# The last blocks of a two-layer token kernel in 512 columns, its phase-A buffers moved to the far end of SBUF, and its short tail loads issued by GpSimd

## The chip, the core and the metric

One core of a Trainium2 chip runs the kernel. The metric is the device time of one execution in microseconds (us). Engines: PE is TensorE (matmuls; PEld is its weight load), DVE is VectorE, ACT is ScalarE, POOL is GpSimd, SP is SyncE, which here only issues DMAs.

## What is computed

```python
def _attn_ref(q, k, v, omega):          # q, k, v: (4, 8, 576, 64); omega: (128, 64)
    scale = 1.0 / np.sqrt(np.sqrt(D))
    def phi(x):
        proj = np.einsum('bhsd,md->bhsm', x, omega)
        h = proj - np.sum(x * x, axis=-1, keepdims=True) / 2.0
        h = h - np.max(h, axis=-1, keepdims=True)
        return np.exp(h) / np.sqrt(m)
    q_p, k_p = (phi(q * scale), phi(k * scale))
    kv = np.einsum('bhsm,bhsd->bhmd', k_p, v)
    z = np.sum(k_p, axis=2)
    num = np.einsum('bhsm,bhmd->bhsd', q_p, kv)
    den = np.einsum('bhsm,bhm->bhs', q_p, z)[..., None] + 1e-06
    return num / den
# x: the attention output as 2304 tokens x 512
x = (x @ w_a) * (x @ w_b) @ w_out       # 512 -> 1536 -> 512   (phase A)
h = np.maximum(x @ w_in, 0.0)
out = h * h @ w_out2                    # 512 -> 2048 -> 512   (phase B)
```

Weights arrive as 64-bit floats; the kernel splits each into a high and a low fp32r part on ACT and DVE, does the same with the activations, and takes three products (high-high, high-low, low-high) for each matmul.

## The kernel before

**Attention.** Per batch of 576 tokens and pair of heads, 512 tokens are taken as four chunks of 128 (`Side`, `k_steps`, `q_steps`), and the last 64, the tail, of four heads at a time apart (`kt_steps`, `qt_steps`; tiles `kt`, `qt`, `VT`). `tail_load` and `kt_steps` issue four DMAs of 32 KB for each tail tile of a batch: twelve such sets, 48 DMAs, all on SP's queue. `kt_steps` runs ahead of the two `k_steps` of its group; `kv_tail` is added to each. The lanes of attention are cut into steps and woven (`merge`, `chain`, `SIDES`) into phase A's units, and a scheduler then orders each engine's instructions by their place in the program.

**Phase A** (`a_units`) works on nine blocks of N = 256 tokens. A unit (block, f), with f one of FA = 12 slices of 128 of the 1536 features, has 12 matmuls into one half of a PSUM bank for `w_a` (three terms times KC = 4 slices of 512), 12 into the other half for `w_b`, the product on ACT and DVE (`a_s`, `gs`: lines 599 to 602), and, LAG = 2 units later, 12 matmuls of `w_out` into the two `y` banks (`outs`, line 562). `PASSES` lists the order: blocks 0 to 2 by halves of f, blocks 3 to 6 whole, and the last two blocks, 7 and 8, by halves again, so that half of the first-layer weights is done with, and their slots can take second-layer weights, before phase A ends. A half pass parks its sum in DRAM (`y_d`) and the next reads it back (`prefetch`, `y_p`).

**Second-layer weights** (`get_w2`) are 32 tiles: each a 512 KB load (`raw`, two buffers), five DVE and three ACT instructions (`split`), into a slot. 20 of them are made during the last four passes, 12 in phase B's first two passes.

**Phase B** (`b_units`) takes the same nine blocks of 256. For each of FB = 16 slices f: 12 matmuls `ph` of 256 columns (line 673), relu, square and split on ACT and DVE (lines 680 to 683), and, LAGB = 2 slices later, per 128 tokens three matmuls `o` whose moving operand is the 512 columns of `wo2` (line 661), six for a block. So `ph`, `ab` and `y` stream 256 columns, and `o` streams 512. The last rows are copied out on ACT (`o_s`) and stored.

## Time and profile before

| | |
|---|---|
| median of 3 executions | 1091.64 us (1089.7 to 1091.91) |
| the profiled execution | 1089.11 us, span from first to last instruction 1087.3 us |
| mean granted TensorE clock | 0.997 |
| PE busy | 1056.3 us, 7705 matmuls |
| DVE, ACT busy | 575.8 us, 514.0 us |
| 40 slices, busy tenths, PE | 5998999999999999999999999999999999999998 |
| the same, DVE | 4888887666655433454467877623333323333322 |
| matmuls `ab`, `ph`, `o`, `y` | 2592, 1728, 864, 1296 |

Each digit is the busy share of a fortieth of the span in tenths. Busy spans of PE overlap since matmuls are pipelined, so a full digit doesn't mean that PE is at its fastest: what one matmul costs in a stream is the distance from one start to the next.

### The profile page before, as it was taken

The page shows a single profiled execution, that of the slowest core. Times are in us where ns is not written, and L with a number is a line of the kernel's source. Part 1 is how long each engine was busy: PE and PEld are TensorE (multiplying, and loading weights), DVE is VectorE, ACT ScalarE, POOL GpSimd, SP SyncE. Part 2 cuts the span into 40 slices and gives each one's busy share as a digit, 9 for nine tenths or more (in the row PEclk, how much of TensorE's full clock was granted, in tenths as well). Part 3 has the DMA queues.
Part 4 walks back from the last instruction along what each step waited for, and adds up shares of the span by engine and source line. Part 5 has one row for each costly group of instructions (what it writes and reads, how often), then busy time and mean ns, then how long its engine had stood idle before and what let it go on. Part 6 is the DMA issues. An engine that isn't in the chain of part 4 may idle for free.

```text
span 1087.3 us, 19942 instructions
## 1 busy us (share of the span) xinstructions
PE 1056.3 (97%) x7705; PEld 991.1 (91%) x7705; DVE 575.8 (53%) x1700; ACT 514.0 (47%) x1321; POOL 0.7 (0%) x6
## 2 busy tenths in 40 slices
PE   5998999999999999999999999999999999999998
PEld 3797989999999999999999998999999999999997
DVE  4888887666655433454467877623333323333322
ACT  4887767654465533433346654523332323323232
POOL 0000000000000000000000000000000000000000
...
GB/s 138 195 200 175 236 255 186 237 201 88 156 132 95 97 135 112 127 98 113 121 136 266 276 285 258 78 1 40 39 28 12 40 1 39 20 2 20 1 20 20
DMA packets 109630, 127.19 MB, mean 117 GB/s; under 512 B 62176, under 2 KB 82656, under 8 KB 109536
## 3 DMA queue, kind: packets, MB, share of 16 engines
...
q8 instruction: 61, 1.00, 0.4%
...
## 4 chain that ended last, share of the span: by engine, by line
PE 88%; DMA 3%; DVE 3%; ACT 3%; issue 1%; SPq 1%; ACTq 0%
PE ab L548 25%; PE ph L673 19%; PE o L661 18%; PE y L562 12%; PE ps_p L289 3%; PE ps_p L222 3%; PE ps_kv L356 2%; PE ps_n L413 2%; PE ps_qt L405 2%; DMA raw<-in_moe_w_out_dram 2%; PE ps_t L267 1%; DVE u L138 1%; PE ps_x L423 1%; ACT a L124 1%; DVE p L129 1%
## 5 line engine op out<-in xcount | busy, mean ns | idle before, releaser
L548 PE MATMUL ab<-x,w 128*128 128x256 f32 x2592 | 368.4, 289 | 1.3 <-ACT x L485 1.3
L548 PEld LDWEIGHTS ab<-x,w 128*128 128x128 f32 x2592 | 332.3, 192 | 2.9 <-ACT x L485 1.5
L673 PEld LDWEIGHTS ph<-yx,w 128*128 128x128 f32 x1728 | 223.8, 192 | 10.0
L673 PE MATMUL ph<-yx,w 128*128 128x256 f32 x1728 | 226.8, 283 | 0.0
L661 PE MATMUL o<-w,ss 128*128 128x512 f32 x864 | 219.0, 393 | 0.0
L562 PE MATMUL y<-gs,wo 128*128 128x256 f32 x1296 | 187.9, 290 | 2.8 <-ACT gs L601 2.2
L661 PEld LDWEIGHTS o<-w,ss 128*128 128x128 f32 x864 | 154.5, 189 | 26.5
L562 PEld LDWEIGHTS y<-gs,wo 128*128 128x128 f32 x1296 | 167.5, 192 | 4.2 <-ACT gs L601 2.6
L681 DVE TENSOR_TENSOR r<-r 128x256 f32<-128x256 f32 x144 | 61.3, 426 | 199.1 <-ACT r L680 196.7
L680 ACT ACTIVATE r<-ph 128x256 f32<-128x256 f32 x144 | 55.5, 385 | 186.5 <-PE ph L673 186.5
L683 DVE TENSOR_TENSOR ss<-r,ss 128x256 fp32r<-128x256 f32 x144 | 61.4, 426 | 63.2 <-PE o L661 48.8
L682 ACT CAST ss<-r 128x256 fp32r<-128x256 f32 x144 | 58.7, 408 | 65.4 <-DVE r L681 65.4
L599 ACT ACTIVATE a_s<-ab 128x256 f32<-128x256 f32 x108 | 41.4, 383 | 90.4 <-PE ab L548 90.2
L600 DVE TENSOR_TENSOR a_s<-ab,a_s 128x256 f32<-128x256 f32 x108 | 45.4, 420 | 45.8 <-ACT a_s L599 45.1
L124 ACT ACTIVATE a<-raw 128x512 f32<-128x512 f32 x68 | 46.4, 683 | 30.9 <-DMA raw<-in_moe_w_in_dram 9.9
L601 ACT CAST gs<-a_s 128x256 fp32r<-128x256 f32 x108 | 44.0, 408 | 28.8 <-DVE a_s L600 28.1
L296 DVE CUSTOM_DVE_ANT_0 c<-ps_p,c 128x128 f32<-128x128 f32 x160 | 39.7, 287 | 28.2 <-ACT c L294 27.8
L602 DVE TENSOR_TENSOR gs<-a_s,gs 128x256 fp32r<-128x256 f32 x108 | 45.5, 421 | 11.9 <-ACT gs L601 10.3
L138 DVE SCALAR_TENSOR_TENSOR u<-raw,u 128x512 uint32<-128x512 uint32 x68 | 46.6, 686 | 0.8 <-ACT u L134 0.3
L129 DVE SCALAR_TENSOR_TENSOR p<-a,p 128x512 int32<-128x512 int32 x68 | 46.7, 686 | 0.6
L134 ACT ACTIVATE u<-raw 128x512 int32<-128x512 uint16 x68 | 46.1, 678 | 0.0
L294 ACT COPY c<-ps_p 128x256 f32<-128x256 f32 x80 | 28.7, 372 | 35.1 <-PE ps_p L289 34.1
...
## 6 DMA issues: line engine op xcount, KB each, us to landing
...
y_d<-y_s SPq DMA_DIRECT2D x18, 256.0 KB, 4.5
yraw<-y_d SPq DMA_DIRECT2D x18, 256.0 KB, 2.9
```

Of the source, the lines that this page charges most:

```text
L124: nc.scalar.activation(out=a, in_=f32(up), func=ACTF.Copy, scale=WORD_SCALE)
L129: nc.vector.scalar_tensor_tensor(out=i32(p), in0=i32(a), scalar=-0x80000000, in1=i32(p), op0=ALU.bitwise_and, op1=ALU.bitwise_or,)
L134: nc.scalar.activation(out=i32(u), in_=raw.bitcast(U16)[:, :, 1], func=ACTF.Copy, scale=2.0 ** 7,)
L138: nc.vector.scalar_tensor_tensor(out=u.bitcast(U32), in0=up.bitcast(U32), scalar=23, in1=u.bitcast(U32), op0=ALU.logical_shift_left, op1=A ...
L548: nc.tensor.matmul(ps, lhsT=wv[:, s_, kc, :], rhs=x[:, kc, m_, :], start=(kc == 0 and (s_, m_) == TERMS[0]), stop=(kc == KC - 1 and (s_, m ...
L562: nc.tensor.matmul(y[c // 2][:, c % 2, :], lhsT=wo[pi, f][:, s_, c * 128:(c + 1) * 128], rhs=g[:, m_, :],  start=(f == f0 and c % 2 == 0 a ...
L661: nc.tensor.matmul(op[t], lhsT=s_t[f][:, s_, t * 128:(t + 1) * 128], rhs=wo2[f][:, m_, :], start=(f == 0 and (s_, m_) == TERMS[0]), stop=( ...
L673: nc.tensor.matmul(ps, lhsT=wv[:, s_, kc, :], rhs=y[:, kc, m_, :], start=(kc == 0 and (s_, m_) == TERMS[0]), stop=(kc == KC - 1 and (s_, m ...
L680: nc.scalar.activation(out=r, in_=ps, func=ACTF.Relu, scale=1.0 / W_SCALE)
L681: nc.vector.tensor_tensor(out=r, in0=r, in1=r, op=ALU.mult)
L682: nc.scalar.copy(out=s_t[f][:, 0, :], in_=r)
L683: nc.vector.tensor_tensor(out=s_t[f][:, 1, :], in0=r, in1=f32(s_t[f][:, 0, :]), op=ALU.subtract)
```

## The change

**Two blocks at once.** The last entry of `PASSES` is now one pass over blocks 7 and 8 together with all twelve f. Its matmuls stream 512 columns (`x_all[:, x0:x0 + 2]`); `w_a`, `w_b` and each of the four `y` parts have a PSUM bank of their own (banks 4 to 7 and 0 to 3), and `outs` follows one unit behind instead of two. The half passes of these blocks, with their parked sums, are gone. Phase B takes the blocks as `BB`: four of 512 columns and one of 256, `outs` one slice behind.

**Places.** `xpool`, `wop` and `gpool` lie at the right end of SBUF and close when phase A ends; `x_all` is one tile with three places instead of three buffers. `w2l`, `wide` and `yl` take the left end that attention leaves; `w2r` and `yr` take the right end after phase A. 27 of the 32 second-layer weights (`get_w2`) are made during the wide pass, most of them in first-layer slots as each f is done with, and five in phase B's first block.

**Tails.** The 48 tail DMAs are issued by GpSimd. `k_lane` runs `kt_steps` merged with the first `k_steps` of its group; the tail's product is added after that one, so ACT copies twice 130 columns where it copied 260 once.

```diff
+    pa = ExitStack()
+    xpool = pa.enter_context(tc.tile_pool(name="xpool", bufs=1, side="right"))
+    wop = pa.enter_context(tc.tile_pool(name="wop", bufs=3, side="right"))
+    gpool = pa.enter_context(tc.tile_pool(name="gpool", bufs=3, side="right"))
...
+    y_d = [
+        dram.tile([128, KC, min(2, NBLK - i) * N], F32, name=f"y_d{i // 2}")
+        for i in range(0, NBLK, 2)
+    ]
...
+    x_all = xpool.tile([128, 3, KC, 2, N], F32R, name="x_all")
 
     def x_tile(i):
-        if i not in xs:
-            xs[i] = xpool.tile([128, KC, 2, N], F32R, tag="x", name=f"x{i}")
-        return xs[i]
+        return x_all[:, i % 3]
...
-                    nc.sync.dma_start(
+                    nc.gpsimd.dma_start(
                         out=t[64 * e:64 * e + ST, g],
                         in_=src[b, h0:h0 + 2, SM:S, :].rearrange("h t d -> t h d"),
                     )
...
         st = tail_turn("k", b, g)
         yield
+        yield
         kp = ap1.tile([128, 2, M], F32, tag="kpt", name="kpt")
         phi_wide(st, kp)
         yield
+
+        while (b, g) not in kv_raw:
+            yield
         ps = at_bank([128, 2, 2, D + 1], "ps_kt")
         for h in range(2):
             nc.tensor.matmul(
                 ps[:, h].rearrange("p e d -> p (e d)"), lhsT=kp[:, h, :],
                 rhs=VT[:, g, h].rearrange("p e d -> p (e d)"), start=True, stop=True,
             )
-        t = ap2.tile([128, 2, 2, D + 1], F32, tag="kvt", name="kvt", bufs=1)
+        t = ap2.tile([128, 2, D + 1], F32, tag="kvt", name="kvt", bufs=1)
         kv_tail[b, g] = t
-        nc.scalar.copy(out=t, in_=ps)
-        kv_raw[b, g] = ap2.tile([128, 2, 2, D + 1], F32, tag="kvr", name="kvr", bufs=NP)
+        kv = kv_raw[b, g][:, :, 0, :]
+        nc.scalar.copy(out=t, in_=ps[:, :, 1, :])
+        nc.vector.tensor_tensor(out=kv, in0=ps[:, :, 0, :], in1=kv, op=ALU.add)
         yield
...
+        if e == 0:
+            kv_raw[b, g] = ap2.tile([128, 2, 2, D + 1], F32, tag="kvr", name="kvr", bufs=NP)
+            nc.scalar.copy(out=kv_raw[b, g][:, :, 0, :], in_=ps)
+        else:
+            nc.vector.tensor_tensor(
+                out=kv_raw[b, g][:, :, 1, :], in0=ps, in1=kv_tail[b, g], op=ALU.add
+            )
...
-            for x in ([(kt_steps(b, p // 2), 4)] if p % 2 == 0 else []) + [(k_steps(b, p), 7)]
+            for x in [merge((k_steps(b, p), 7), *([(kt_steps(b, p // 2), 7)] if p % 2 == 0 else []))]
...
-    PASSES += [(i, FH, FA) for i in (NBLK - 2, NBLK - 1)]
+    PASSES = [((i,), 0, FH) for i in range(3)] + [((i,), FH, FA) for i in range(3)]
+    PASSES += [((i,), 0, FA) for i in range(3, NBLK - 2)]
+    PASSES += [((NBLK - 2, NBLK - 1), 0, FA)]
     wa, wb, wo = {}, {}, {}
     LAG = 2
+    wide_pool = []
...
+            if wide:
+                for c in range(KC):
+                    t = ypool.tile([128, 2, N], F32, tag="ys", name="y_s")
+                    nc.scalar.mul(out=t, in_=yp[pi][c], mul=1.0 / W_SCALE ** 2)
+                    for x, i in enumerate(bl):
+                        nc.sync.dma_start(out=y_cols(i)[:, c, :], in_=t[:, x, :])
+                return
...
+            bl = PASSES[pi][0]
+            wide = len(bl) == 2
+            if wide:
+                x0 = bl[0] % 3
+                x = x_all[:, x0:x0 + 2]
+                aps, bps = (bank(4 + (2 * f + z) % 4, [128, 2, N], "abw") for z in range(2))
+                gp, w_ = wide_pool[0], 2 * N
+            else:
+                x = x_tile(bl[0])
+                ab = bank(2 + n % (2 if pi <= AT_END else 6), [128, 2, N], "ab")
+                aps, bps = ab[:, 0, :], ab[:, 1, :]
+                gp, w_ = gpool, N
+            proj(aps, wa[f], x)
             yield pi, f, "a"
-            proj(ab[:, 1, :], wb[f], x)
-            a_s = gpool.tile([128, N], F32, tag="t", name="a_s")
-            g = gpool.tile([128, 2, N], F32R, tag="gs", name="gs", bufs=3)
+            proj(bps, wb[f], x)
...
+            pending.append((pi, f))
+            while len(pending) > (1 if wide else LAG):
+                outs(*pending.pop(0))
             yield pi, f, "o"
-        for n in range(len(todo) - LAG, len(todo)):
-            outs(*todo[n])
+        for x in pending:
+            outs(*x)
...
+    BB = [(i * N, min(2, NBLK - i) * N) for i in range(0, NBLK, 2)]
+    ys = {}
+
+    def y_load(i, pool):
+        w_ = BB[i][1]
+        t = pool.tile([128, KC, 2, w_], F32R, tag="yx", name=f"yx{i}")
+        ys[i] = t
+        for c in range(KC):
+            r = ypool.tile([128, w_], F32, tag="ys", name="yraw")
+            nc.sync.dma_start(out=r, in_=y_d[i][:, c, :])
+            nc.scalar.copy(out=t[:, c, 0, :], in_=r)
...
+            for t in range(w_ // 128):
+                if f == 0:
+                    op[t] = bank(t, [128, DM], f"o{t}")
...
+        gp = wide_pool[0]
+        for f in range(FB):
+            ps = bank(4 + f % 4, [128, w_], "ph")
+            wv = wi2[f].rearrange("p a (k f) -> p a k f", k=KC)
+            for kc in range(KC):
...
+            r = gp.tile([128, w_], F32, tag="t", name="r")
+            s_t[f] = gp.tile([128, 2, w_], F32R, tag="gs", name="ss")
...
+            if f:
+                outs(f - 1)
             yield f
...
+        outs(FB - 1)
...
+    W2_L, W2_R = 3, 2 * (FB - FA) - 3
+    w2 = {"n": 0}
...
-        x, f = w2_list.pop(0)
-        po = (w2[0], "w2") if f < FB - FA else (wpool, "w")
+        w2["n"] += 1
+        x, f = w2_list[n]
+        if n < W2_L:
+            po = (w2["l"], "w2")
+        elif n < W2_L + 2 * FA:
+            po = (wpool, "w")
...
+            w2["l"] = ctx.enter_context(tc.tile_pool(name="w2l", bufs=W2_L))
+            wide_pool.append(ctx.enter_context(tc.tile_pool(name="wide", bufs=2)))
+            w2["yl"] = ctx.enter_context(tc.tile_pool(name="yl", bufs=1))
...
+            if w2["n"] < W2_L + 2 * f + (2 if kind != "a" else 0):
+                get_w2()
+            if f == 4 and kind == "o":
+                y_load(0, w2["yl"])
         u += 1
         while done < min(n_side, u * n_side / (n_units * FR.get(pi, 1.0))):
...
+        for f in b_units(i):
+            get_w2()
+            if f == (4 if i == 0 else FB - 6) and i + 1 < len(BB):
+                y_load(i + 1, w2["yl" if i % 2 else "yr"])
 
 
 # ---- launch: one core; inputs and outputs as the reference has them ----
```

What the scheduler makes of it, at three places. First SP's queue at the start of the program: `om` is omega, `kt` and `VT` are tails, `kn` and `V` the 512 tokens of a pair of heads, `raw` a weight. Before:

```order
L175 DMA om<-in_omega_dram 128x64
L176 DMA om<-in_omega_dram 128x64
L203 DMA kt<-in_k_dram 64x2x64 x4
L317 DMA VT<-in_v_dram 64x2x64 [waits DVE_49]
L317 DMA VT<-in_v_dram 64x2x64
L317 DMA VT<-in_v_dram 64x2x64 [waits DMAHW0_49]
L317 DMA VT<-in_v_dram 64x2x64 [waits DMAHW1_49]
L103 DMA raw<-in_moe_w_a_dram 128x4x256 [waits DMAHW2_49]
L247 DMA kn<-in_k_dram 128x8x64 [waits DMAHW3_49]
L342 DMA V<-in_v_dram 128x8x64 [waits DMAHW4_49]
```

Now:

```order
L179 DMA om<-in_omega_dram 128x64
L180 DMA om<-in_omega_dram 128x64
L251 DMA kn<-in_k_dram 128x8x64
L351 DMA V<-in_v_dram 128x8x64 [waits DVE_49]
L107 DMA raw<-in_moe_w_a_dram 128x4x256
L107 DMA raw<-in_moe_w_b_dram 128x4x256
L254 DMA qn<-in_q_dram 128x2x64 x2
```

The eight tail loads ahead of `raw` and `kn` have left SP's queue, and `kn` and `V` stand ahead of the first weights.

Second ACT's first instructions, where `OMS`, `OMZ` and `OM` are copies of the transposed omega, which every feature projection needs, and `S` and `T` are copies of transposed tokens and tails. Before:

```order
L187 ACT_TABLE_LOAD
L187 ACTIVATE OMS<-ps_om 128x128 [waits PE_49]
L190 ACTIVATE OMZ<-ps_om 64x128 [waits DVE_49]
L190 ACTIVATE OMZ<-ps_om 64x128
L191 CAST OM<-OMS 128x128 [waits Activation_49]
L215 COPY T<-ps_tt 128x128 [waits PE_49]
L124 ACTIVATE a<-raw 128x512 [waits DMAHW2_49]
L134 ACTIVATE u<-raw 128x512
L273 COPY S<-ps_t_176 128x512 [waits PE_49]
```

Now:

```order
L128 ACT_TABLE_LOAD
L128 ACTIVATE a<-raw 128x512 [waits DMAHW4_49]
L191 ACTIVATE OMS<-ps_om 128x128 [waits PE_49]
L194 ACTIVATE OMZ<-ps_om 64x128 [waits DVE_49]
L194 ACTIVATE OMZ<-ps_om 64x128
L195 CAST OM<-OMS 128x128 [waits Activation_49]
L138 ACTIVATE u<-raw 128x512
L277 COPY S<-ps_t_156 128x512 [waits PE_49]
L137 CAST w<-p 128x512 [waits DVE_49]
L219 COPY T<-ps_tt 128x128 [waits PE_49]
```

The scaling of the first weight, which waits for a DMA, now stands ahead of the copies of omega, and `S` ahead of `T`.

Third ACT's queue from phase A into phase B: `gs` and `ss` are the high parts that `y` and `o` of PE wait for, `y_s` copies a finished sum out of PSUM, `r` is the relu of `ph`. Before:

```order
L601 CAST gs<-a_s 128x256 [waits DVE_49]
L133 CAST w<-p 128x512 [waits DVE_49]
L124 ACTIVATE a<-raw 128x512 [waits DMAHW6_49]
L134 ACTIVATE u<-raw 128x512
L680 ACTIVATE r<-ph 128x256 [waits PE_49,Activation_49]
L124 ACTIVATE a<-raw 128x512 [waits DMAHW7_49,DVE_49]
L134 ACTIVATE u<-raw 128x512
L682 CAST ss<-r 128x256 [waits DVE_49]
```

Now:

```order
L597 ACTIVATE y_s<-y_8021 128x512 [waits PE_49]
L128 ACTIVATE a<-raw 128x512 [waits DMAHW1_49,DVE_49]
L597 ACTIVATE y_s<-y_8022 128x512 [waits PE_49]
L137 CAST w2r<-p 128x512 [waits DVE_49]
L138 ACTIVATE u<-raw 128x512
L137 CAST w2r<-p 128x512 [waits DVE_49]
L597 ACTIVATE y_s<-y_8023 128x512 [waits DMAHW2_49,DMAHW3_49,PE_49,Activation_49]
L723 ACTIVATE r<-ph 128x512 [waits PE_49]
L128 ACTIVATE a<-raw 128x512 [waits DMAHW4_49,DVE_49]
L138 ACTIVATE u<-raw 128x512
L597 ACTIVATE y_s<-y_8024 128x512 [waits DMAHW6_49,DMAHW5_49,Activation_49]
L725 CAST ss<-r 128x512 [waits DVE_49]
```

Four copies of sums, two of which wait for DMAs as well, now stand among the weight splits ahead of the first `ss`.

## Rows read from the trace of the kernel before

**Rows 1.** Engines by stage: stretch, length, busy us (instructions) of each, clock, DMA share.
```profile
0.00:12.24 12.24, 0.89 (x2) 0.36 (x3) 2.52 (x7) 3.74 (x8) 0.70 (x6) 1.00 0.49 110
12.24:190.00 177.76, 166.09 (x1193) 151.15 (x1194) 148.11 (x437) 135.12 (x368) 0.00 (x0) 0.99 0.72 204
...
561.00:676.85 115.85, 113.07 (x926) 112.06 (x925) 91.54 (x190) 70.47 (x142) 0.00 (x0) 0.99 0.81 265
676.85:1083.00 406.15, 406.15 (x2594) 369.54 (x2593) 140.93 (x323) 135.76 (x329) 0.00 (x0) 1.00 0.08 25
```

**Rows 2.** Timeline of PE in phase B: start, us from first start to last end.
```profile
898.71 4.27 PE L661 MATMUL o<-w,ss 128*128 128x512 f32 x18
...
902.82 4.48 PE L673 MATMUL ph<-yx,w 128*128 128x256 f32 x36
...
907.13 1.55 PE L661 MATMUL o<-w,ss 128*128 128x512 f32 x6
...
909.95 1.55 PE L661 MATMUL o<-w,ss 128*128 128x512 f32 x6
```

**Rows 3.** Timeline of PE in phase A without attention.
```profile
563.91 1.60 PE L562 MATMUL y<-gs,wo 128*128 128x256 f32 x12
565.35 3.04 PE L548 MATMUL ab<-x,w 128*128 128x256 f32 x24
568.23 1.60 PE L562 MATMUL y<-gs,wo 128*128 128x256 f32 x12
```

**Rows 4.** Timeline of the first 15 us; in brackets the engine's idle time before, and what ended it.
```profile
1.65 2.70 SPq L203 DMA_DIRECT2D kt<-in_k_dram  x4
...
4.38 0.30 ACT L191 CAST OM<-OMS 128x128 fp32r<-128x128 f32 x1
...
6.99 0.59 SPq L103 DMA_DIRECT2D raw<-in_moe_w_a_dram  x1
7.63 0.63 SPq L247 DMA_DIRECT2D kn<-in_k_dram  x1
...
11.05 0.66 ACT L124 ACTIVATE a<-raw 128x512 f32<-128x512 f32 x1 [5.45 <-DMA raw<-in_moe_w_a_dram]
...
12.24 0.69 PE L267 MATMUL ps_t<-ident,kn 128*128 128x128 f32 x2 [6.94 <-DMA kn<-in_k_dram]
...
14.25 0.59 ACT L273 COPY S<-ps_t 128x512 f32<-128x512 f32 x1 [1.97 <-PE ps_t L267]
```

**Rows 5.** Timeline of PE from phase A into phase B.
```profile
669.87 0.38 PE L562 MATMUL y<-gs,wo 128*128 128x256 f32 x1 [0.21 <-ACT gs L601]
670.52 1.57 PE L562 MATMUL y<-gs,wo 128*128 128x256 f32 x11 [0.26 <-DVE gs L602]
674.08 3.19 PE L562 MATMUL y<-gs,wo 128*128 128x256 f32 x12 [1.99 <-ACT gs L601]
677.06 4.92 PE L673 MATMUL ph<-yx,w 128*128 128x256 f32 x36
```

**Rows 6.** The stretch after that wait, columns as in the first group.
```profile
674.60:678.10 3.50, 3.50 (x17) 3.50 (x17) 2.95 (x6) 1.51 (x3) 0.00 (x0) 0.51 0.49 154
```

**Rows 7.** DMA issues: count, KB each, median us to landing (part 6 of the page).
```profile
y_d<-y_s SPq DMA_DIRECT2D x18, 256.0 KB, 4.5
```

**Rows 8.** Groups of 561 to 676.85 us: count, busy us, mean ns, idle time before.
```profile
L146 DVE SCALAR_TENSOR_TENSOR w<-u,a 128x512 fp32r<-128x512 uint32 x27 | 18.6, 689 | 2.2 <-PE ab L548 1.8
L124 ACT ACTIVATE a<-raw 128x512 f32<-128x512 f32 x27 | 18.3, 676 | 18.6 <-DMA raw<-in_moe_w_out_dram 9.5 <-DMA raw<-in_moe_w_in_dram 7.1 <-DVE a L142 1.6
...
L142 DVE TENSOR_SCALAR a<-p 128x512 int32<-128x512 int32 x26 | 11.0, 422 | 0.1
```

**Rows 9.** Line 213, the turns of the tails: what PE waited for.
```profile
L213 PE MATMUL ps_tt<-ident,kt x8: 272/273/445, 4.9 to 338.7; 128*128 128x128 f32 x8
...
  DMA kt<-in_k_dram: 2.8, 2
```

**Rows 10.** Line 429, the last writes of `x`: min, median, max ns, first and last start.
```profile
L429 DVE TENSOR_TENSOR x<-ps_x,x x40: 281/422/427, 32.8 to 560.8; 128x256 fp32r<-128x256 f32 x24, 128x128 fp32r<-128x128 f32 x16
```

More of the change, by code (lines that the diff above doesn't have):

```diff
@@ L552, in proj, with y_cols, y_part @@
                     )
+        def y_cols(i):
+            o = i % 2 * N
+            return y_d[i // 2][:, :, o:o + N]
+        def y_part(pi, f, c):
+            if len(PASSES[pi][0]) == 2:
+                return yp[pi][c].rearrange("p t n -> p (t n)")
+            return yp[pi][c // 2][:, c % 2, :]
         def outs(pi, f):
-            i, f0, f1 = PASSES[pi]
+            bl, f0, f1 = PASSES[pi]
             g = g_t.pop((pi, f))
+            wide = len(bl) == 2
             if f == f0:
-                yp[pi] = [bank(c, [128, 2, N], f"y{c}") for c in range(KC // 2)]
-            y = yp[pi]
+                yp[pi] = [bank(c, [128, 2, N], f"y{c}") for c in range(KC if wide else KC // 2)]
             for c in range(KC):
@@ L562, in outs @@
                     nc.tensor.matmul(
[L563 removed]
+                        y_part(pi, f, c), lhsT=wo[pi, f][:, s_, c * 128:(c + 1) * 128],
                         rhs=g[:, m_, :],
[L566 to L567 removed]
+                        start=(f == f0 and (wide or c % 2 == 0) and (s_, m_) == TERMS[0]),
+                        stop=(f == f1 - 1 and (wide or c % 2 == 1) and (s_, m_) == TERMS[-1]),
                     )
@@ L644, in out_rows, with b_units @@
         return res
-    op_b = {}
-    def b_units(i, f0, f1):
-        y = xs["y", i]
-        s_t = {}
-        op = op_b.setdefault(i, {})
-        par = 2 * (i % 2)
+    def b_units(i):
+        y = ys[i]
+        c0, w_ = BB[i]
+        s_t, op = {}, {}
         def outs(f):
-            for t in range(N // 128):
-                if t not in op:
-                    op[t] = bank(par + t, [128, DM], f"o{t}")
+            for t in range(w_ // 128):
+                if f == 0:
+                    op[t] = bank(t, [128, DM], f"o{t}")
                 for s_, m_ in TERMS:
@@ L665, in outs @@
                     )
-        for f in range(f0, f1 + LAGB):
-            if f < f1:
-                ps = bank(4 + f % 4, [128, N], "ph")
-                wv = wi2[f].rearrange("p a (k f) -> p a k f", k=KC)
-                for kc in range(KC):
-                    for s_, m_ in TERMS:
-                        nc.tensor.matmul(
-                            ps, lhsT=wv[:, s_, kc, :], rhs=y[:, kc, m_, :],
-                            start=(kc == 0 and (s_, m_) == TERMS[0]),
-                            stop=(kc == KC - 1 and (s_, m_) == TERMS[-1]),
-                        )
-                r = gpool.tile([128, N], F32, tag="t", name="r")
-                s_t[f] = gpool.tile([128, 2, N], F32R, tag="gs", name="ss", bufs=3)
-                nc.scalar.activation(out=r, in_=ps, func=ACTF.Relu, scale=1.0 / W_SCALE)
-                nc.vector.tensor_tensor(out=r, in0=r, in1=r, op=ALU.mult)
-                nc.scalar.copy(out=s_t[f][:, 0, :], in_=r)
-                nc.vector.tensor_tensor(
-                    out=s_t[f][:, 1, :], in0=r, in1=f32(s_t[f][:, 0, :]), op=ALU.subtract
-                )
-            if f >= f0 + LAGB:
-                outs(f - LAGB)
+        gp = wide_pool[0]
@@ new lines, in b_units @@
+        for f in range(FB):
+            ps = bank(4 + f % 4, [128, w_], "ph")
+            wv = wi2[f].rearrange("p a (k f) -> p a k f", k=KC)
+            for kc in range(KC):
+                for s_, m_ in TERMS:
+                    nc.tensor.matmul(
+                        ps, lhsT=wv[:, s_, kc, :], rhs=y[:, kc, m_, :],
+                        start=(kc == 0 and (s_, m_) == TERMS[0]),
+                        stop=(kc == KC - 1 and (s_, m_) == TERMS[-1]),
+                    )
+            r = gp.tile([128, w_], F32, tag="t", name="r")
+            s_t[f] = gp.tile([128, 2, w_], F32R, tag="gs", name="ss")
+            nc.scalar.activation(out=r, in_=ps, func=ACTF.Relu, scale=1.0 / W_SCALE)
+            nc.vector.tensor_tensor(out=r, in0=r, in1=r, op=ALU.mult)
+            nc.scalar.copy(out=s_t[f][:, 0, :], in_=r)
+            nc.vector.tensor_tensor(
+                out=s_t[f][:, 1, :], in0=r, in1=f32(s_t[f][:, 0, :]), op=ALU.subtract
+            )
+            if f:
+                outs(f - 1)
```

97 lines of the change are left out of this document (31 added, 66 removed).

## The prediction

> **What bounds the kernel now.** I read the table of engines by stage first: PE is busy in 166.09 of the 177.76 us with attention, in 113.07 of the 115.85 us before the boundary between the phases, and in all of phase B's 406.15 us; DVE and ACT are busy 140.93 and 135.76 us of the latter [rows 1]. So the time is PE's, and a change pays where it takes PE time away, or idle time out of PE's stream.
>
> PE's timeline, by distances from start to start, tells what a matmul costs in a stream, since busy spans overlap. In phase B, 36 `ph` take 907.13 - 902.82 = 4.31 us, 120 ns each with 256 columns; 18 `o` take 902.82 - 898.71 = 4.11 us, 228 ns each with 512 [rows 2]. In phase A, 24 `ab` take 568.23 - 565.35 = 2.88 us, again 120 ns [rows 3]. One matmul of 512 columns is thus 2 x 120 - 228 = 12 ns cheaper than two of 256. Six `o` and one slice's `ph` (12 x 120 = 1.44) take 909.95 - 907.13 = 2.82 us, so six `o` that stand alone take 1.38, 230 each; the 12 more in the run of 18 took 4.11 - 1.38 = 2.73, 227.5 each. I take 227.5 inside a run, and 15 ns for each change of run; 230 for all is the pessimistic end.
>
> **Part 1, wider blocks.** In phase B, two blocks' slice now costs 2 x 2.82 = 5.64 us. After: 12 `ph` and 12 `o` of 512 columns, 24 x 0.2275 + 0.015 = 5.475, a saving of 0.165. There are 4 wide blocks of 16 slices: 64 x 0.165 = **10.6 us**. In phase A, two blocks' unit has 72 matmuls of 256, 2 x 4.32 = 8.64 us, and becomes 36 x 0.2275 = 8.19: 12 units x 0.45 = **5.4 us**. Together 16.0. With 230 ns for all 768 + 432 = 1200 merged matmuls it is 12.0, with the run's lower end about 17.
>
> The Trainium skill, "TensorE: Matmul & The Clock Gate", section "Back-to-back issue gap", speaks against this part: it puts the isolated gap of warm matmuls at N / 2.4 + 2.5 ns, so a merged pair would save 2.5 ns and the 1200 an estimated 3.0 us. The trace disagrees: both [rows 2] and [rows 3] give 120 ns at 256 columns, where that rule gives 109. The same section's figures for a stream with weight loads, 81 ns at 128 columns and 131 at 512, lie far from 228 too.
>
> **Part 2, the start.** Before, SP spends 1.65 to about 7 us on eight tail issues, so `raw` is issued at 6.99 and `kn` at 7.63. PE idles 6.94 us until `kn` lands at 12.24 (4.6 us after issue), and the first `S` is ready at 14.25 + 0.59 = 14.84 [rows 4]. After, `kn` goes out at about 1.65 and lands at 6.3, `raw` goes out after `kn` and `V` (0.63 and some 0.7), near 3.0, and lands by 7.1 to 7.6 (before, its first reader started at 11.05, 4.1 after issue). But ACT's queue now has the scaling of `raw` first, so `OMS`, `OMZ` and `OM`, which only need omega, are queued behind that DMA, and with them every first projection. Serial sum on ACT: 7.6 + 0.66 (L124) + 4 copies x 0.30 (L191) + 0.66 (the second scaling, at L124's price) + 0.59 (`S`) = 10.7 [rows 4]. Gain **4.1 us**; bounds 0, if the tails or the weights then fall due first, and 6.0, the whole lead of `kn`. Other lanes' order in the next 178 us changes too; PE idles 11.7 us there [rows 1], and I carry 0 with 4 us either way.
>
> **Part 3, tails.** The 48 issues leave SP, which is no bound except at the start. What a DMA issued by GpSimd costs, no row of before shows. In program order each set is issued when the last reader of its buffer is done, tens of PE instructions ahead of use, and PE waited for tails 2.8 us in two instances before [rows 9]. I take 0; the bounds are -2.8 (those waits vanish) and an exposure that the last rival prices.
>
> The Trainium skill, "SBUF — State Buffer", section "SBUF: two separate sides", warns that descriptors of GpSimd-issued DMAs cannot be written while DVE holds a shared port in one of its fast modes, and advises SP or ACT as issuer. That would make these tails late while DVE is busy; no run here shows it yet.
>
> **Part 4, between the phases.** Before, the last sums drain through waits of 0.21, 0.26 and 1.99 us [rows 5], and after that 3.50 us run at a granted clock of 0.51 [rows 6], the lower of 1.2 and 2.4 GHz: 3.50 x 0.49 = 1.7 us lost. In all 4.2. After, the last `outs` needs `gs` of one unit earlier only at its own turn, but ACT must then drain four `y_s` in two buffers. The first two stores land 4.5 us after issue [rows 7]; with T the end of the last `y` and 0.7 for each part's three matmuls, the first part is done at T - 2.1 and its copy ends near T - 1.4, so the third copy waits till T + 3.1, starts by 3.7, and then `r`, two scalings, the fourth copy (0.6 to 0.7 each) stand ahead of `ss`, ready near T + 6.9. PE has 24 `ph` until T + 5.5 and then stalls 1.4. If the clock drops again that is 3.1 in all, a gain of **1.1 us**; bounds -2 (the copies wait longer) and +4.2 (no stall). At the very end the last `outs` is one slice behind instead of two and waits for the chain of ACT and DVE on its `ph`: **-0.3**, 0 to -1.
>
> **Part 5, 27 weights under the wide pass.** A split costs DVE three instructions of 689 ns and two of 422 [rows 8], 2.91 us; a wide unit has two splits and two instructions of its own at 689, 7.2 us of 8.19. The first three units have three splits, 10.1 us: DVE falls 3 x 1.9 = 5.7 us behind. `gs` is needed one unit after `ab`, 8.19 us less a chain of two ACT and two DVE instructions (2.7) = 5.5 us of cushion. That about covers it: **-1.0**, bounds 0 and -5. The last write of `x` by attention started at 560.8 [rows 10], so the wide pass, which begins later, doesn't wait for it.
>
> **Sum**: 16.0 + 4.1 + 1.1 - 0.3 - 1.0 = 19.9. The profiled execution took 1089.1, so 1069.2; the median of the runs is 2.5 above that execution, which leaves 0 to 2.5 upward. I say **1069**.
>
> **Rivals.**
> (a) The start gains nothing, so the change doesn't do there what it says: the head of ACT's queue waits longer for `raw`, or the first tail, which PE's row 16 needs, lands after 14 us. For: two of the first things on ACT and POOL now wait or are new. Against: `raw` is issued 4 us earlier. 1069.2 + 4.1 = 1073.3.
> (b) Splits pace the wide pass. Before, 27 splits took 115.85 us, 4.29 each, with ACT idle 18.6 ahead of the first scaling, 16.6 of it for `raw` [rows 8]; the wide pass has 98 us for as many. DVE works in order, so a late `raw` holds up `gs`. Against: that stretch's DMA share of 0.81 [rows 1] held parked sums and twice the `wo` loads, which are gone, and phase B needs the last weights only late. 5 to 17.5 us more: 1074 to 1087.
> (c) Width saves nothing: `ph`, `ab` and `y` of 512 columns start 240 ns apart, as two of 256 do, because what made `o` cheap lies in its operands (a weight moves and an activation is loaded; in the others it is the reverse) and not in its width. Then the 16.0 goes: 1085.2. Against: `o` and `ph` load a weight each alike, and [rows 2] and [rows 3] find one price for `ph`, `ab` and `y` at 256, whatever their operands. By the rule of the Trainium skill's page "TensorE: Matmul & The Clock Gate" above it would be an estimated 13.0 less gain, 1082.2.
> (d) Slower: GpSimd's tails are late at each of twelve sets. PE's stream there has no other work ready behind a `ps_tt`, since PE runs in order. The change loses as a whole from 19.9 / 12 = 1.7 us exposed a set; at the 2.8 / 2 = 1.4 of [rows 9] it would almost tie, and at 2.5 it is 12 x 2.5 = 30 us, 1099. Against: the sets are issued far ahead.
>
> **Chances**: forecast 0.60, (a) 0.13, (b) 0.12, (c) 0.04, (d) 0.11. The range 1060 to 1083 takes in the forecast's bounds (start +1.9, boundary +3.1, order +4, so 1060), (a), (c) and most of (b), and leaves out (d). A measurement here tells about 0.2%, 2.2 us, from no change: faster 0.86, same 0.04 (the mild ends of (b) and (d)), slower 0.10.
>
> **What would show it.** In the changed profile: `ph` and `ab` of 512 columns starting 227 ns apart, a wide slice of phase B 5.47 us long and a wide unit 8.19; the first scaling heading ACT's idle time, `S` ready near 10.7; PE waiting about 1.4 us for `ss` some 5.5 us after the last `y`, with a granted clock near 0.5 behind it; waits for `gs` of under a few us in the wide pass's first units, with DVE at nine tenths; no wait of PE for `kt`, `qt` or `VT` above a us. A wide matmul at 240 ns, PE waiting on `gs` throughout the wide pass, or twelve waits for tails would make me wrong, each by the term named.

## The result, and where the time went

The changed kernel takes 1077.07 us (median of 4 executions, 1075.23 to 1081.43) against 1090.67 us before in the same comparison (1088.7 to 1091.91): ratio 0.9883, 95% interval 0.9862 to 0.9905, so 10 to 15 us faster. The forecast was 1069 with a range of 1060 to 1083: right way, inside the range, but the gain is 13.6 us where some 20 were reckoned.

The profiled execution took 1076.06 us, its span is 1074.3 us, 13.0 less than before. First the page's head and engines by stage (columns as in [rows 1]; the second line's stretch is the wide pass, the third is phase B):

```profile
span 1074.3 us, 17147 instructions
...
PE 1047.3 (97%) x6505; PEld 928.2 (86%) x6505; DVE 554.1 (52%) x1546; ACT 487.4 (45%) x1179; POOL 29.2 (3%) x54
```

```profile
11.80:190.00 178.20, 168.95 (x1215) 155.23 (x1216) 150.01 (x446) 138.56 (x383) 18.02 (x31) 0.96 0.67 197
562.78:666.70 103.92, 103.92 (x459) 83.94 (x458) 85.96 (x160) 63.16 (x110) 0.00 (x0) 1.00 0.67 209
666.70:1070.50 403.80, 401.02 (x1825) 328.31 (x1823) 119.17 (x192) 112.97 (x204) 0.00 (x0) 1.00 0.08 25
```

PE is still the bound. I take the ledger by three marks in PE's stream, before and after: the first `ab` of blocks 7 and 8's pass (565.35 and 562.78), the first `ph` (677.06 and 666.70), PE's end (1083.30 and 1070.51).

| stretch | before | after | gained |
|---|---|---|---|
| start to the last pass | 565.35 | 562.78 | 2.6 |
| last pass of phase A | 111.71 | 103.92 | 7.8 |
| phase B | 406.24 | 403.81 | 2.4 |
| after PE's end | 4.0 | 3.8 | 0.2 |

Phase B stands out: the forecast had 10.6 us there from width alone. PE's timeline shows why. Block 0, then block 1, which has the same instructions with other tiles:

```profile
698.11 2.88 PE L716 MATMUL ph<-yx,w 128*128 128x512 f32 x12
700.83 2.88 PE L704 MATMUL o<-w,ss 128*128 128x512 f32 x12
...
797.72 2.98 PE L716 MATMUL ph<-yx,w 128*128 128x512 f32 x12
800.53 2.92 PE L704 MATMUL o<-w,ss 128*128 128x512 f32 x12
803.29 2.98 PE L716 MATMUL ph<-yx,w 128*128 128x512 f32 x12
```

In block 0 twelve matmuls take 2.72 us, 226.7 ns each; [rows 2] gave 228 for `o`. In block 1 `ph` takes 2.81 (234) and `o` 2.76 (230). Blocks 0 and 2 keep 226.7 up to f = 12, blocks 1 and 3 are above it throughout. So is the wide pass as a whole, 24 `abw` in 5.61 us (234) and 12 `y` in 2.81 (234):

```profile
604.86 5.77 PE L561 MATMUL abw<-x_all,w 128*128 128x512 f32 x24
610.47 2.98 PE L585 MATMUL y<-gs,wo 128*128 128x512 f32 x12
613.28 5.76 PE L561 MATMUL abw<-x_all,w 128*128 128x512 f32 x24
```

Summed against 226.7 ns, matmuls that start further apart cost 2.8 us in the wide pass and 4.9 in phase B. A second loss is at the ends of phase B's blocks; between block 3 and block 4 PE and ACT look like this:

```profile
1018.23 5.76 PE L704 MATMUL o<-w2r,ss 128*128 128x512 f32 x24
...
1021.93 1.30 ACT L735 ACTIVATE o_s<-o 128x512 f32<-128x512 f32 x2 [1.47 <-PE o L704]
...
1025.87 0.60 ACT L735 ACTIVATE o_s<-o 128x512 f32<-128x512 f32 x1 [2.65 <-DMA out_dram<-o_s]
1026.37 0.38 ACT L723 ACTIVATE r<-ph 128x256 f32<-128x256 f32 x1
...
1027.69 1.66 PE L704 MATMUL o<-w,ss 128*128 128x512 f32 x6 [0.84 <-ACT ss L725]
```

The third `o_s` waits 2.65 us for a store to free one of two buffers, with the next block's `r` and `ss` behind it in ACT's queue, and PE idles for `ss`. From the wide pass to the end PE waits for nothing else, 2.8 us in four places, one of them the boundary between the phases:

```profile
PE o L704 <- ACT ss L725: 2.8, 4, 1.0
```

With the matmuls just after them, the four block ends cost 3.6 us and the boundary 1.8.

### The profile page after: what moved, and what is told of

Its sections match the earlier page's. It is cut to its first block, busy times and chain, and to the rows that moved or that the text cites. A ratio compares the mean times of both kernels' runs of the same rounds, so it can differ in the third digit from the quotient of the medians.

```text
span 1074.3 us, 17147 instructions
## 1 busy us (share of the span) xinstructions
PE 1047.3 (97%) x6505; PEld 928.2 (86%) x6505; DVE 554.1 (52%) x1546; ACT 487.4 (45%) x1179; POOL 29.2 (3%) x54
## 3 DMA queue, kind: packets, MB, share of 16 engines
q0 software_dynamic: 1536, 1.58, 0.6%
## 4 chain that ended last, share of the span: by engine, by line
PE 90%; DMA 3%; ACT 3%; DVE 2%; issue 1%; SPq 0%; ACTq 0%
PE ab L561 22%; PE o L704 18%; PE ph L716 17%; PE y L585 13%; PE abw L561 6%; PE ps_p L293 3%; PE ps_n L426 3%; PE ps_kv L365 3%; PE ps_p L226 2%; PE ps_qt L418 2%; DMA out_dram<-o_s 1%; PE ps_t L271 1%; DMA raw<-in_moe_w_b_dram 1%; PE ps_x L436 1%; DMA raw<-in_moe_w_a_dram 1%
## 5 line engine op out<-in xcount | busy, mean ns | idle before, releaser
L561 PE MATMUL ab<-x_all,w 128*128 128x256 f32 x2016 | 298.0, 292 | 0.4 <-DVE x_all L499 0.3
L561 PEld LDWEIGHTS ab<-x_all,w 128*128 128x128 f32 x2016 | 263.8, 191 | 2.1 <-DVE x_all L499 0.5
L716 PE MATMUL ph<-yx,w 128*128 128x512 f32 (+1 forms) x840 | 185.5, 371 | 0.0
L585 PE MATMUL y<-gs,wo 128*128 128x256 f32 (+1 forms) x1152 | 181.4, 302 | 0.0
L704 PE MATMUL o<-w,ss 128*128 128x512 f32 x702 | 172.5, 392 | 2.8 <-ACT ss L725 2.8
L716 PEld LDWEIGHTS ph<-yx,w 128*128 128x128 f32 x840 | 148.1, 188 | 29.5
L724 DVE TENSOR_TENSOR r<-r 128x512 f32<-128x512 f32 (+1 forms) x80 | 51.1, 638 | 225.3 <-ACT r L723 225.3
L726 DVE TENSOR_TENSOR ss<-r,ss 128x512 fp32r<-128x512 f32 (+1 forms) x80 | 51.1, 639 | 48.0 <-ACT ss L725 41.9
L561 PE MATMUL abw<-x_all,w 128*128 128x512 f32 x288 | 69.2, 395 | 0.0
L561 PEld LDWEIGHTS abw<-x_all,w 128*128 128x128 f32 x288 | 53.9, 188 | 13.0
```

What stands on the lines that cost most here:

```text
L561: nc.tensor.matmul(ps, lhsT=wv[:, s_, kc, :], rhs=x[..., kc, m_, :], start=(kc == 0 and (s_, m_) == TERMS[0]), stop=(kc == KC - 1 and (s_, ...
L585: nc.tensor.matmul(y_part(pi, f, c), lhsT=wo[pi, f][:, s_, c * 128:(c + 1) * 128], rhs=g[:, m_, :],  start=(f == f0 and (wide or c % 2 == ...
L704: nc.tensor.matmul(op[t], lhsT=s_t[f][:, s_, t * 128:(t + 1) * 128], rhs=wo2[f][:, m_, :], start=(f == 0 and (s_, m_) == TERMS[0]), stop=( ...
L716: nc.tensor.matmul(ps, lhsT=wv[:, s_, kc, :], rhs=y[:, kc, m_, :], start=(kc == 0 and (s_, m_) == TERMS[0]), stop=(kc == KC - 1 and (s_, m ...
L724: nc.vector.tensor_tensor(out=r, in0=r, in1=r, op=ALU.mult)
L726: nc.vector.tensor_tensor(out=s_t[f][:, 1, :], in0=r, in1=f32(s_t[f][:, 0, :]), op=ALU.subtract)
```

## Experiments

Each experiment's ratio is against the kernel before on the same chip; the changed kernel's own is 0.9883. Executions of the changed kernel and its variants scatter by some 4 us to either side, once by 7, so differences under 0.2% to 0.3% are not told apart by the time, and the trace of each is read for its place.

**Is it the width that gains?** Every wide `ab`, `y`, `ph` as two of 256 columns:

```diff
-    nc.tensor.matmul(ps, lhsT=wv[:, s_, kc, :], rhs=y[:, kc, m_, :], ...)
+    for z in range(w_ // N):
+        nc.tensor.matmul(ps[:, z * N:(z + 1) * N], lhsT=wv[:, s_, kc, :],
+                         rhs=y[:, kc, m_, z * N:(z + 1) * N], ...)
```

> The changed kernel with each wide ab, y and ph (512 columns) issued as two matmuls of 256 columns with the same weight into the two halves of the bank; all else as it is. Theory (width gains): ab, y, ph start 119 to 120 ns apart; the wide pass costs 12 x (72 x 0.120 - 36 x 0.2333) = 2.9 us more, phase B 64 x 12 x (2 x 0.1195 - 0.2267) = 9.4 us less the 3 us that the slow wide ones lost: some 9 more in all, 1086. Rival (the gain is not from width but from passes that are gone and the start): within 2 of 1077.

1086.05 us, ratio 0.9969 (0.9947 to 0.9991): 9.4 us of the gain gone, 9 expected. Its PE timeline:

```profile
605.89 5.92 PE L563 MATMUL abw<-x_all,w 128*128 128x256 f32 x48
611.65 3.01 PE L588 MATMUL y<-gs,wo 128*128 128x256 f32 x24
614.50 5.92 PE L563 MATMUL abw<-x_all,w 128*128 128x256 f32 x48
```

48 take 5.76 us, 120.0 each, as [rows 3] had it. By the spans of the two traces the loss is 7.9 us (1082.2 against 1074.3). So width is most of the gain, by the mechanism forecast: a merged pair saves 2 x 120.0 - 226.7 = 13.3 ns. The rule of the Trainium skill ("TensorE: Matmul & The Clock Gate", section "Back-to-back issue gap"; N / 2.4 + 2.5 ns), by which width would have brought an estimated 3 us, does not fit this stream.

**Why do some wide matmuls take longer?** The dear matmuls have an operand among the tiles that the change placed from the right end of SBUF: `x_all`, `wo`, `yx1`, `yx3`, `w2r`. (An exception is `o` in blocks 1 and 3, at 230 with `w` and `ss` from the left: by the single starts in block 1 the first eight after a run of dear `ph` lie 224 to 236 ns apart and the last four 226 to 227, so the disturbance runs on for some matmuls.) First theory: the place itself. One run maps places, the other moves all tiles of phase B and of the wide pass below 192 KB:

```diff
-    rawp = ctx.enter_context(tc.tile_pool(name="rawp", bufs=2))
+    rawp = ctx.enter_context(tc.tile_pool(name="rawp", bufs=2, side="right"))
...
-    w2["yr"] = ctx.enter_context(tc.tile_pool(name="yr", bufs=1, side="right"))
+    w2["yr"] = ctx.enter_context(tc.tile_pool(name="yr", bufs=1))
```

(and so for `cutp`, `ypool` and `w2r`, with `xpool` as the innermost of the right pools).

> This kernel leaves out all of the computation: it is only streams of 24 fp32r matmuls, first of 512 columns (wide), then of 256 (narrow), for 7 x 7 pairs of places in SBUF of the moving operand (first letter) and the loaded weight (second letter): A, B, C, D, E, F, G at 24, 104, 152, 172, 184, 196, 212 KB from the start of each partition; and one stream whose moving operand is two pieces of 256. No other engine works beside it. In the changed kernel, wide matmuls start 226.7 ns apart in phase B's blocks 0 and 2, whose operands all lie below 177 KB, and 229.8 to 234.6 in the wide pass and in blocks 1 and 3, where one operand lies above 188 KB. Theory (place): pairs with one letter of A to D and the other F or G start about 233 apart, pairs of A to D 226.7, and pairs with both high near 227; narrow ones 120 everywhere. Rival (traffic): the slow stretches come from weight splits and DMAs beside them; then all wide pairs here take 226.7. Rival (shape): the moving operand in two pieces makes the wide pass slow; then only the last stream is at 233.

> The changed kernel with only places changed: the buffers of weight splitting and of sums (raw, u, a, p, y_s) lie at the right end, and every tile that a matmul of the wide pass or of phase B reads lies below 192 KB; the order of instructions on each engine is the same. Theory (place): the wide pass loses its 2.8 us above 226.7 ns a matmul, phase B its 0.46 + 2.13 + 0.41 + 1.91 = 4.9 us; 7.7 less than the changed kernel, about 1069.4, and all wide runs at 226.7. Rival (traffic): no change, 1077.

In the map every one of the 49 wide pairs of places takes 5.44 us for 24, 226.7 ns, and every narrow one 120; the operand in two pieces 228. Neither place nor shape matters by itself. Yet with the tiles moved, 1072.65 us, ratio 0.9848 (0.9827 to 0.9868, which overlaps the changed kernel's), phase B is at 226.7 in every block and 3.1 us shorter as a whole (400.70 against 403.82), and the wide pass, against the theory, keeps its 233:

```profile
604.47 5.77 PE L561 MATMUL abw<-x_all,w 128*128 128x512 f32 x24
610.08 2.98 PE L585 MATMUL y<-gs,wo 128*128 128x512 f32 x12
...
797.66 2.88 PE L716 MATMUL ph<-yx,w 128*128 128x512 f32 x12
800.38 2.88 PE L704 MATMUL o<-w,ss 128*128 128x512 f32 x12
```

Traffic falls as a cause too, since instructions and their order are the same. What differs are the start addresses in the compiled program. (No trace shows them. Their differences agree with the tile sizes in the code: `x_all` with its 24576 bytes and the five `w2r` with 20480 both end at 229344.) In the changed kernel, `w`, `yx0`, `ss` and the wide `gs`, placed from the left, start at multiples of 128 bytes (16512, 163968, 155776), while `x_all`, `wo`, `yx1` and `w2r` start 96 bytes past one (204768, 192480, 192480, 208864). With the tiles moved, `x_all` and `wo` (158688, 183264) still do, and nothing of phase B does. Second theory: the offsets of the two operands within 32, 64 or 128 bytes. A map of offsets, and 32 or 96 unused bytes at the right end:

```diff
     pa = ExitStack()
+    ctx.enter_context(tc.tile_pool(name="padp", bufs=1, side="right")).tile([128, 24], F32, name="pad")
```

> This kernel leaves out all of the computation: streams of 24 fp32r matmuls as in the map of places, with the moving operand (first letter) and the weight (second letter) starting at 0 (A), 32 (B), 64 (C) or 96 (D) bytes past a multiple of 128 bytes; wide is 512 columns, narrow 256. In the map of places, where all starts were multiples of 64 bytes, every wide pair took 226.7 ns, so the place as such is not it. In the changed kernel the slow stretches are those with x_all, wo, yx1, yx3 and w2r, whose starts lie 32 bytes past a multiple of 64; after moving all of phase B to multiples of 64 it ran at 226.7, while the wide pass, still at 32 past, stayed at 233. Theory (32 bytes): wide pairs with B or D in either letter take 230 to 235, the others 226.7; narrow ones change by under 2 ns. Rival (it needs real data or traffic): 226.7 for all.

> The changed kernel with 32 unused bytes at the right end of SBUF, so that everything placed from that end starts at a multiple of 64 bytes; the instructions and their order are the same. Theory (32 bytes): the wide pass and all of phase B at 226.7 ns a matmul: 2.8 + 4.9 = 7.7 us less than the changed kernel's profile, about 1069. Rival (it is how far up in SBUF the tiles lie): the wide pass stays at 233, blocks 1 and 3 at 230 to 235, no change of time, 1077.

> The changed kernel with 96 unused bytes at the right end instead of none: everything placed from that end then starts at a multiple of 128 bytes, as everything from the left end does. Same instructions and order. Theory (a wide matmul takes 226.7 ns where both operands start at the same offset within 128 bytes, 229 to 234 where not, as the map of offsets showed): every run of the wide pass and of phase B's wide blocks at 226.7 to 227, also ab and y, which had 229.4 and 233.4 with 32 bytes; 7.7 us less than the changed kernel's profile, 21 less than the kernel before. Rival (multiples of 64 were the point, the rest comes from DMAs beside): ab and y stay at 229 to 233.

PE's timeline of the map of offsets (first letter the moving operand's offset, second the weight's; A 0, B 32, C 64, D 96 bytes):

```profile
27.91 5.61 PE L57 MATMUL wideAA<-big 128*128 128x512 f32 x24
33.36 5.75 PE L57 MATMUL wideAB<-big 128*128 128x512 f32 x24
38.95 5.76 PE L57 MATMUL wideAC<-big 128*128 128x512 f32 x24
44.55 5.77 PE L57 MATMUL wideAD<-big 128*128 128x512 f32 x24
50.16 5.76 PE L57 MATMUL wideBA<-big 128*128 128x512 f32 x24
55.76 5.61 PE L57 MATMUL wideBB<-big 128*128 128x512 f32 x24
61.21 5.75 PE L57 MATMUL wideBC<-big 128*128 128x512 f32 x24
...
72.40 5.67 PE L57 MATMUL wideCA<-big 128*128 128x512 f32 x24
77.91 5.76 PE L57 MATMUL wideCB<-big 128*128 128x512 f32 x24
...
94.55 5.76 PE L57 MATMUL wideDA<-big 128*128 128x512 f32 x24
```

Next start less start, by 24: AA (33.36 - 27.91) / 24 = 227 ns, BB 227, and likewise CC and DD; AB, AC, AD, BA, BC 233 to 234; CA (77.91 - 72.40) / 24 = 230, and DB 229. So it isn't the multiple of 64 that I had expected, since BB and DD take 227: what counts is whether both operands start at the **same** offset within 128 bytes. The narrow pairs go the other way, 119 to 120 where equal, 114 to 120 where not, so the kernel before could show nothing of it.

With 32 bytes `x_all`, `wo` and `yx1` come to 64 past a multiple of 128. The map then foretells CA, 230 ns, for `abw`, and AC, 233, for `y`:

```profile
607.54 5.67 PE L561 MATMUL abw<-x_all,w 128*128 128x512 f32 x24
613.04 2.96 PE L585 MATMUL y<-gs,wo 128*128 128x512 f32 x12
615.84 5.67 PE L561 MATMUL abw<-x_all,w 128*128 128x512 f32 x24
```

That is 5.50 / 24 = 229 and 2.80 / 12 = 233, neither the 226.7 of this run's theory nor its rival's unchanged 233 for both. With 96 bytes all are equal, and all take 227, in phase B as well:

```profile
604.88 5.60 PE L561 MATMUL abw<-x_all,w 128*128 128x512 f32 x24
610.32 2.88 PE L585 MATMUL y<-gs,wo 128*128 128x512 f32 x12
613.04 5.60 PE L561 MATMUL abw<-x_all,w 128*128 128x512 f32 x24
```

The times: 32 bytes 1074.46 us, ratio 0.9838 (0.9814 to 0.9862); 96 bytes 1073.24 us, ratio 0.9822 (0.9794 to 0.9849), which is 6.7 us beyond the changed kernel's ratio where 7.7 were expected. The profiled executions differ by less, 1075.27 against 1076.06 us: the wide pass is 2.7 us shorter, but phase B takes 404.52 us against 403.82, so that in this trace it gives back all that equal offsets gained there.

```profile
665.10:1069.62 404.52, 399.71 (x1825) 330.63 (x1823) 119.28 (x193) 113.34 (x205) 0.00 (x0) 0.99 0.08 25
673.00:677.20 4.20, 4.20 (x12) 3.11 (x11) 4.05 (x8) 2.59 (x6) 0.00 (x0) 0.60 0.64 180
```

The boundary takes 4.1 us over 226.7 ns a matmul instead of 1.8, the block ends 7 instead of 3.6. PE waits 4.6 us for `ss` in all instead of 2.8, and behind two of these waits, of 1.7 and 1.8 us, the granted clock falls: 0.60 in the second line's stretch, 0.53 from 1025.4 to 1029.0, where matmuls start up to 427 ns apart. Why the waits are longer is open; with the tiles moved, and the wide pass as slow as before, they came to 4.1 us too. What equal offsets are worth in phase B is seen in runs whose block ends cost nothing: 400.95 us with four `o_s` alone, 396.42 with the 96 bytes as well (the run without the new start, below; it also has four `y_s` and later splits, and idles 1.3 us at the boundary, as the other does 1.2).

**The ends of blocks.** Four buffers for `o_s`:

```diff
-            o = cutp.tile([128, DM], F32, tag="a", name="o_s")
+            o = w2["os"].tile([128, DM], F32, tag="os", name="o_s")      # pool of 4
```

> The changed kernel with four buffers of their own for o_s instead of two shared with the splits. Theory (ACT's queue at the ends of phase B's blocks: the third and fourth o_s wait for the stores of the first two, ahead of the next block's r and ss): the idle before the first o of a block (0.30, 0.62, 0.84 us) and the slow stretch after it go, 2.5 to 3.5 us less, about 1074. Rival (PE waits there for the ordinary chain ph, r, ss): idle stays, 1077.

1076.88 us, ratio 0.9858 (0.9833 to 0.9882), 2.7 us beyond the changed kernel's. In the trace PE's only wait from the wide pass on is the boundary's:

```profile
PE o L704 <- ACT ss L725: 1.2, 1, 1.2
```

The four block ends took 4.6 us over 226.7 ns a matmul in the changed kernel (offsets included), 1.5 here. The stores are no faster (the first two of each block land after 3.6 to 4.1 us, in the changed kernel after 2.8 to 4.4), so it is the buffers. The intervals of the times overlap; the traces settle this one, and the two other traces with four buffers (under "All together") have no wait at a block's end either.

How much two buffers cost depends on the stores. With the tails on SP (the run below), ACT's instructions in phase B and their order are the same as in the changed kernel, but the first two stores of each block land after 2.0 to 2.6 us, the third `o_s` waits less, PE waits at no block's end, and phase B takes 400.48 us:

```profile
1027.68 0.60 ACT L735 ACTIVATE o_s<-o 128x512 f32<-128x512 f32 x1 [1.47 <-DMA out_dram<-o_s]
```

Why the stores land sooner there is open.

**The boundary between the phases.** Four buffers for the last `y_s`:

```diff
-                    t = ypool.tile([128, 2, N], F32, tag="ys", name="y_s")
+                    po, tag = (gpool, "gs") if c < 3 else (ypool, "ys")
+                    t = po.tile([128, 2, N], F32, tag=tag, name="y_s")
```

> The changed kernel with four buffers instead of two for the last y_s of phase A. Theory (the third and fourth y_s wait for stores, ahead of the first ss): the idle of 0.99 us before the first o of phase B goes, and with it the 1.8 us that the boundary takes over 226.7 ns a matmul shrink to under 0.6. Rival (the splits of weights ahead of ss in ACT's queue do it): idle of 0.5 us or more stays.

The idle stays, at 1.36 us, so the rival holds: ACT's queue has a weight's scaling, waiting for its load, ahead of `ss`.

```profile
675.62 0.66 ACT L128 ACTIVATE a<-raw 128x512 f32<-128x512 f32 x1 [1.61 <-DMA raw<-in_moe_w_in_dram]
...
677.39 3.38 PE L705 MATMUL o<-w,ss 128*128 128x512 f32 x12 [1.36 <-ACT ss L726]
```

In the run without the new start (below), which has these four buffers too, ACT waits 1.58 us for the same load and PE idles 1.34; with all four changes it waits for no load there, and PE idles 0.17. (The one execution of this run took 1083.6 us; a single one does not place it.)

**The start and the tails.** The 48 loads back on SP; and, apart, only the first four `kt` on SP, with the first weight a little later:

```diff
-                    nc.gpsimd.dma_start(
+                    (nc.sync if (nm, b) == ("k", 0) else nc.gpsimd).dma_start(
...
-    S0, SD = 1, 12
+    S0, SD = 3, 12
```

> The changed kernel with the 48 tail loads back on SP's queue; the scheduler then puts omega's copies ahead of the first weight's scaling on ACT, and the tails between the first tokens and the first weight on SP. Theory (ACT's head bounds the start): the first projection starts near 7.2 instead of 11.8 us, since only kn is waited for, and the first weight, some 5 us later, isn't needed yet: 4 us less than the changed kernel, about 1073. Rival (the tails' place on GpSimd is what gained at the start): the first projection starts later than 11.8 and it takes 3 us more, 1080. Rival (GpSimd's late tails cause the idle of 1.8 us at 85 and 1.6 us at 153): these go, 3 us less.

> The changed kernel with the first four kt loads on SP and the first weight's load a little later, which brings omega's copies, S and T ahead of the first weight's scaling in ACT's queue. Theory (ACT's queue behind the first weight's load bounds the start): the first projection starts near 7.2 instead of 11.8, the first ps_kv near 12 instead of 15.9, and the whole is 3 to 4 us shorter, 17 less than the kernel before. Rival (the lead is lost further on, where PE waits for other loads and the granted clock falls): the first projection starts near 7.2, but the time stays within 1 us, 13 to 14 less than before.

Tails on SP: 1075.42 us, ratio 0.985 (0.9827 to 0.9874), no slower than the changed kernel. The first projection starts at 7.23 us as expected, but the exponentials `kp` then stand behind the first weight's scaling:

```profile
12.32 0.66 ACT L128 ACTIVATE a<-raw 128x512 f32<-128x512 f32 x1 [4.58 <-DMA raw<-in_moe_w_a_dram]
...
13.86 1.20 PE L365 MATMUL ps_kv<-V,kp 128*128 128x65 f32 x4 [2.84 <-ACT kp L232]
```

So the head of ACT's queue does bound the start. What the issuer of the tails is worth for the whole, the time does not tell, since the trace has two differences of opposite sign: the last pass begins at 568.21 instead of 562.78, with a granted clock of 0.84 in the first 40 us against 1.00, and phase B is 3.3 us shorter by the stores above. The idle time near 153 us stays (PE is busy in 12.70 of the 15 us from 150 to 165, against 12.68), so late tails are not its cause. With `om_first` the first projection starts at 8.70 and the first `ps_kv` at 12.98 instead of 15.87, but the last pass begins at 564.44, later than the changed kernel's 562.78, and the granted clock of the first 60 us is 0.91 instead of 1.00. 1078.37 us, ratio 0.9856 (0.9832 to 0.988): between theory and rival, not settled.

**All together.** 96 bytes, four `o_s`, four `y_s` with the last splits later, and the start of `om_first`; then the same with the changed kernel's own start:

> The changed kernel with what the other runs point to: 96 bytes at the right end, four o_s buffers, four buffers for the last y_s with the last five weights' splits later in phase B's first block, and the start as in om_first. Theory (the parts add up): 7.7 + 3 + 0.5 + 0 to 4 less than the changed kernel, 25 to 29 us less than the kernel before. Rival (they share one loss): no more than the 96 bytes alone, 21 less.

> The same as all_four, but with the changed kernel's own start (tails of the first batch on GpSimd, first weight early). In all_four and om_first the first projection came 3 us earlier, yet the last pass of phase A began 1.7 and 4.7 us later than in the changed kernel (564.4 and 567.5 against 562.8), with the granted clock at 0.89 to 0.91 in the first 60 us against 1.00. Theory (the new start costs more than it brings): the last pass begins within 1.5 us of 562.8, and the time is 1 to 4 us under all_four's ratio to the kernel before, 0.971 to 0.974. Rival (the start is neutral and the difference is the chip's scatter): the ratio is 0.975 again, within 0.0015.

All four: 1067.21 us, ratio 0.975 (0.9729 to 0.9772), 25 to 29 us under the kernel before expected, 25.6 measured by the medians; this beats both kernels. Without the new start: 1066.87 us, ratio 0.9784 (0.976 to 0.9808), its last pass begins at 563.63. Its first sign came true, the time didn't: the ratio is not below 0.975, so the theory that the new start costs more than it brings falls. The rival's sign, within 0.0015 of 0.975, failed as well: the two medians differ by 0.3 us, but the kernel before took 2.7 us more beside the first. Whether the new start brings anything is open.

## Why the prediction was right and wrong, step by step

**The price of width** held: 120.0 ns for 256 columns, 226.7 for 512, and with narrow matmuls 9.4 us of the gain go. Rival (c) is out: even at unequal offsets a merged pair saves 240 - 234 = 6 ns, at equal ones 13.

**The step that failed** is in part 1: "I take 227.5 inside a run", for all 1200 merged matmuls. The matmuls in [rows 2] show that price for `o` alone, whose tiles by the map lay at equal offsets; the change put one operand of the wide pass and of half of phase B at another offset, and the rows had no such case. Its term is 16.0 as forecast less 2.8 and 4.9. The pessimistic end of 230 ns was too low as well, since these take up to 234.

**A term was missing**: the ends of phase B's blocks. Part 4 reckoned that `y_s` waits for stores in two buffers with `ss` behind; the same stands at each block of phase B, where four `o_s` now share the two buffers that two shared before, and I didn't look. In this trace it is 3.6 us, in the one with the tails on SP next to nothing. Both steps together are 11.3 us here. That 1077 still lies inside the range is in part luck: the terms in the next paragraph, priced too dear, made up for some of it.

**What was reckoned too dear** gave back about half: 226.7 instead of 227.5 and no loss at a change of run (some 2.6 us); the boundary, 1.8 us instead of 3.1, with a stall of 0.99 where 1.4 was forecast and no fall of the clock; and the wide pass, where DVE is busy 85.96 of 103.92 us, a little under the nine tenths forecast, and PE never waits for `gs` (0 instead of 1.0). Rival (b), splits that pace the wide pass, is out with that. The boundary in the trace of after:

```profile
669.78 0.60 ACT L597 ACTIVATE y_s<-y 128x512 f32<-128x512 f32 x1 [1.58 <-DMA y_d<-y_s]
...
672.87 0.61 ACT L725 CAST ss<-r 128x512 fp32r<-128x512 f32 x1
...
673.54 3.20 PE L704 MATMUL o<-w,ss 128*128 128x512 f32 x12 [0.99 <-ACT ss L725]
```

`ss` starts 6.2 us after the last `y` (666.70) and ends at 6.8; the forecast put its end at 6.9.

**The start** went as told, a little smaller: 3.1 us instead of 4.1, since `raw` landed at 8.99 and not by 7.6. Rival (a) is out.

```profile
3.20 0.86 SPq L107 DMA_DIRECT2D raw<-in_moe_w_a_dram  x1
...
8.99 0.66 ACT L128 ACTIVATE a<-raw 128x512 f32<-128x512 f32 x1 [6.97 <-DMA raw<-in_moe_w_a_dram]
...
11.17 0.58 ACT L277 COPY S<-ps_t 128x512 f32<-128x512 f32 x1
```

By the first `ab` the lead was 5.6 us (52.44 and 46.80), and by the last pass 2.6. Between, the clock took much of it: 80 to 100 us, before and after (clock is the third number from the end),

```profile
80.00:100.00 20.00, 16.92 (x111) 14.61 (x111) 16.96 (x46) 14.22 (x36) 0.00 (x0) 0.91 0.50 154
```

```profile
80.00:100.00 20.00, 16.18 (x91) 14.27 (x89) 14.17 (x44) 11.80 (x30) 0.00 (x0) 0.74 0.47 150
```

The granted clock there is a mean of its two levels, 1.2 and 2.4 GHz: an estimated 20 x 0.17 = 3.4 us, behind an idle time of 1.8 us of PE at 84.8. From 150 to 165 us it is 1.00 before and 0.89 after, another 1.7. Why the same kind of wait costs more clock in the one than in the other is open; the 4 us either way that I carried for this stretch cover it.

**Tails on GpSimd** were harmless, so rival (d) is out. PE waits for no `kt`, `qt` or `VT`. Before, it had waited less than the prediction read: the 2.8 us in two instances of [rows 9] are one wait near 4.8 us, counted for the weight load (1.51) and for its matmul (1.25). An issue takes 592 ns against SP's 608, the landing 4.0 us against 3.3 in the median for `kt`, and 3.0 against 3.1 for `qt`. The sign of what the Trainium skill warns of ("SBUF — State Buffer", section "SBUF: two separate sides": descriptors locked out by DVE) would be late landings while DVE is busy; the latest of all took 6.5 us, against 5.8 from SP.

```profile
L207 POOL DMA_DIRECT2D kt<-in_k_dram x16: 585/592/717, 1.3 to 180.8; - x16
```
